# A branch hint, an earlier flag, later weight splits and y copies on ScalarE alone, in a kernel of attention, expert routing and a gated layer

## The chip, the cores and the metric

The kernel runs on one core of a Trainium2 chip. The metric is the device time of one execution in microseconds (us), as the median of several runs. Five engines work side by side, each with its own instruction queue: TensorE (PE; its weight loads are PEld), VectorE (DVE), ScalarE (ACT), GpSimd (POOL) and SyncE (SP), which issues DMAs. A name with q behind it (DVEq, SPq) is an instruction that the engine's sequencer handles itself: a wait, a branch, a DMA issue.

## What is computed

Three stages, one after the other, in float32:

```python
attn_out = _attn_ref(q, k, v)                     # 4 batches, 8 heads, 576 positions, 64 wide; two window masks
x = attn_out.transpose(0, 2, 1, 3).reshape(2304, 512)

logits = x @ w_gate                               # 8 experts
for idx in np.argsort(-logits.flatten()):         # greedy: best pairs first
    tok, e = idx // 8, idx % 8
    if assigned[tok] >= 0 or counts[e] >= 288:    # every expert takes 288 tokens
        continue
    assigned[tok] = e; counts[e] += 1
out[mask_e] = np.maximum(x[mask_e] @ w1[e], 0) @ w2[e]

gate = 1 / (1 + np.exp(-(out @ moe2_w_gate)))     # 1536 wide
return (gate * (out @ moe2_w_val)) @ moe2_w_out
```

## The kernel before

**Stages.** Attention runs up to about 105 us of the profiled execution. It writes its rows to the DRAM tensor xrows and leaves the logits on the chip. Routing follows (`Route.settle`, L591 to L609), then the expert phase (`Dense.phase_m`, L857), then the gated layer (`Dense.phase_g`, L984). The program is scheduled by hand: on each engine, instructions run in the order in which they are traced, and the framework adds the waits.

**Routing.** `settle` makes five rounds of a bidding scheme (`update`, `choice`), after which a flag says whether more are needed. `count` (L535) writes the number of tokens of each expert into `TB[:, 0]` and each token's place into `TB[:, 1]`; both, and `idxp`, are parts of one PSUM tile, rmisc. `positions` (L556) turns places into row numbers: VectorE makes tables, 18 matmuls (L575) add them up into `idxp`, and two VectorE instructions (L576, L577) make `rows`. `gather` then issues three indirect DMAs on GpSimd (L793), each bringing 128 rows of x (256 KB) for the first expert, and `check` (L543 to L554, seven VectorE instructions) makes a flag that says whether the five rounds were not enough. Every engine loads the flag (L589) and branches (L605). In the rare path, which these inputs don't take, further rounds and a general search follow, and then `positions` and `gather` again. `warm` (L463) issues filler matmuls on TensorE; W2 is 13 of them.

**Weights of the experts.** There are 64 steps, eight for each of eight experts. A step's weights (512 KB, `fetch`, L736, on SP) land in one of four raw buffers; ScalarE makes the high half (`high`, L742), VectorE the low half (`low`, L747), and the low half frees the raw buffer for a later fetch. Three steps stand ready before the expert phase: their high halves are made ahead of `settle`, and `fill` makes the low halves and fetches three further steps. `fill` stands between `check` and the branch.

**A step of the expert phase** (`phase_m`): perhaps a gather and a turn (L801, L811, L812) for the next expert, then `l1` of step j (12 matmuls, L824; ScalarE's relu, L828; VectorE's low half, L829), `l2` of step j - 2 (12 matmuls, L846, into four PSUM tiles y0 to y3 that exist once), `high` and `low` of step j + 2, `feed`, and a fetch of step j + 6. Behind an expert's last `l2` the four y tiles are copied to the SBUF tile yo, two by VectorE and two by ScalarE (L850), and ScalarE issues the store to DRAM (L851). The next expert's first `l2` writes the same PSUM tiles; between the two lies one `l1`.

**Weights of the gated layer.** `enter(t, p)` (L894) fetches a piece p (512 KB, L752, on SP) and enters it for conversion at step t + 3; `feed` converts it (`conv_g`, L755: four VectorE instructions and one of ScalarE) and splits it a step later (`split_g`, L769: one of each). Nine pieces are needed before `phase_g` begins. Three are entered ahead of `settle` (L1118) for steps 3, 5 and 7; six at steps 3, 9, 15, 21, 27 and 33 of `phase_m`.

Of the kernel before, what the change touches and what calls it, by code (L numbers as in the profile page):

```python
# [18 lines left out]
NT, DM, E, CAP = 2304, 512, 8, 288  # L19
# [349 lines left out]
W0, W1, W2, WA, WB = 10, 8, 13, 6, 5  # L369
# [44 lines left out]
class Route:  # L414
# [138 lines left out]
            nc.vector.tensor_copy(f[:, 1:2], f[:, 2:3])  # L553
        nc.vector.tensor_tensor(out=self.flag, in0=f[:, 0:1], in1=f[:, 1:2], op=ALU.add)  # L554

    def positions(self, rows):  # L556
        nc = self.nc
        S, slot, pg, M2, og = self.S, self.slot, self.pg, self.M2, self.og
        nc.vector.tensor_tensor(out=S, in0=self.TB[:, 1], in1=self.He, op=ALU.mult)
        with nc.allow_low_precision("slot numbers are small integers"):  # L560
            nc.vector.tensor_reduce(out=slot[:, 0], in_=S.rearrange("p e c -> p c e"), axis=AX.X, op=ALU.add)
        nc.vector.tensor_scalar(out=slot[:, 1], in0=slot[:, 0], scalar1=127, scalar2=None, op0=ALU.bitwise_and)
        nc.vector.tensor_scalar(out=slot[:, 2], in0=slot[:, 0], scalar1=-128, scalar2=None, op0=ALU.bitwise_and)
        nc.vector.tensor_copy(pg, slot[:, 1:3])
        pf, gf = pg[:, 0], pg[:, 1]
        nc.vector.tensor_tensor(out=og, in0=gf.unsqueeze(1).to_broadcast([128, NCH, NCH]), in1=self.gid, op=ALU.is_equal)
        nc.gpsimd.tensor_tensor(out=M2[:, 0], in0=og, in1=self.cid, op=ALU.mult)
        nc.scalar.activation(out=M2[:, 1], in_=og, func=AF.Copy, scale=self.pid)
        for c0 in (0, HC):
            nc.vector.tensor_tensor(out=self.G[:, :, c0:c0 + HC], in0=pf[:, c0:c0 + HC].unsqueeze(1).to_broadcast([128, 128, HC]),  # L570
                                    in1=self.tab[:, 4], op=ALU.is_equal)
        M2v = M2.rearrange("p a g c -> p (a g) c")
        out = self.idxp.rearrange("p a g -> p (a g)")
        for c in range(NCH):
            nc.tensor.matmul(out, self.G[:, :, c], M2v[:, :, c], start=(c == 0), stop=(c == NCH - 1))  # L575
        nc.vector.tensor_scalar(out=self.ip, in0=self.idxp, scalar1=128.0 * (NCH - 1), scalar2=None, op0=ALU.min)  # L576
        nc.vector.scalar_tensor_tensor(out=rows, in0=self.ip[:, 1], scalar=127.0, in1=self.ip[:, 0], op0=ALU.min, op1=ALU.add)  # L577

# [12 lines left out]
    def settle(self, rows, gather, fill, segments=(5, 1, 2)):  # L591
        s = 0
        for _ in range(segments[0]):
            self.update(s, s == 0, s == segments[0] - 1)
            self.choice()
            s += 1
        self.count()
        self.warm(W1)
        self.positions(rows)
        gather()  # L600
        self.warm(W2)
        self.check(segments[0], False)
        fill()
        v = self.load_flag()
        with self.tc.If(v > 0):  # L605
            self.more(s, segments[1:])
            self.count()
            self.positions(rows)
            gather()  # L609

    def more(self, s, segments):
        if not segments:
# [112 lines left out]
class Dense:  # L725
# [63 lines left out]
    def gather(self, c):  # L789
        if c not in self.xg:  # L790
            self.xg[c] = self.xgp.tile([128, DM], F32, tag="xg", name="xg")
        t = self.xg[c]
        self.nc.gpsimd.indirect_dma_start(out=t, out_offset=None, in_=self.xrows,  # L793
                                          in_offset=bass.IndirectOffsetOnAxis(ap=self.rows[:, c:c + 1], axis=0))
# [40 lines left out]
    def l2(self, j):  # L835
        nc = self.nc
        e, f = divmod(j, 8)
        wh, wl = self.hl.pop(j)
        hh, hl = self.h.pop(j)
        if e not in self.ya:  # L840
            self.ya[e] = self.out_tiles()
        y = self.ya[e]
        for m in range(4):
            s = slice(512 + 128 * m, 640 + 128 * m)
            for n, (w, x) in enumerate(((wh, hh), (wh, hl), (wl, hh))):
                nc.tensor.matmul(y[m], w[:, s], x, start=(f == 0 and n == 0), stop=(f == 7 and n == 2))  # L846
        if f == 7:
            t = self.yp.tile([128, 4, CAP], F32, tag="yo", name="yo")
            for m in range(4):
                (nc.scalar.copy if m % 2 else nc.vector.tensor_copy)(t[:, m], y[m])  # L850
            nc.scalar.dma_start(out=self.yd[:, :, CAP * e:CAP * e + CAP], in_=t)  # L851
            del self.ya[e], self.xt[e]

    def chunks(self, e):
# [2 lines left out]
    def phase_m(self, ng):  # L857

        J = 8 * E
        nc = self.nc  # L860
        gq = [(f, i) for f in range(ng) for i in range(3)][3:]
        self.ya[0] = self.out_tiles()
        for c, n in zip(self.chunks(0), HEAT):
            self.turn(c)
            for _ in range(n):
                nc.tensor.matmul(self.ya[0][0][:, 0:256], self.identb[:, 0:128], self.identb)
        for j in range(J + LAG):
            e, f = divmod(j, 8)
            if e + 1 < E:
                cs = list(self.chunks(e + 1))  # L870
                if 1 <= f <= len(cs):
                    self.gather(cs[f - 1])
                if 4 <= f < 4 + len(cs):
                    self.turn(cs[f - 4])
            if j < J:
                self.l1(j)
            if j >= LAG:
                self.l2(j - LAG)
            if AHEAD <= j + 2 < J:
                self.high(j + 2)  # L880
                self.low(j + 2)
            self.feed(j)
            if J - 4 <= j < J - 2:
                self.fetch_y(0, j - J + 4)
            if J - 2 <= j < J:
                self.split_y(0, 0, j - J + 2)
            if j + AHEAD + 3 < J and j:
                self.fetch(j + AHEAD + 3)
            if j % 6 == 3 and gq:
                self.enter(j, gq.pop(0))  # L890
        for d in range(LAG, 6):
            self.feed(J + d)
# [134 lines left out]
def body(tc, *args):  # L1027
    with ExitStack() as top:
        program(tc, top, *args)


def program(tc, top, qh, kh, vh, wgate, cst, csb, wm, wgv, out):
    nc = tc.nc
    with tc.manual_schedule():
# [9 lines left out]
        rows = cp.tile([128, NCH], I32, name="rows")  # L1044
        toks = cp.tile([128, NCH], I32, name="toks")
        dn = Dense(tc, raw, wm, wgv)
        with ExitStack() as rt:
# [60 lines left out]
            def gather():  # L1108
                for c in dn.chunks(0):
                    dn.gather(c)  # L1110
# [4 lines left out]
                    dn.fetch(j + 4)  # L1115

            dn.rawg = pool(mring, "rawg", 3, side="right")
            for i in range(3):  # L1118
                dn.enter(2 * i, (0, i))
            r.settle(rows, gather, fill)  # L1120
            r.tokens(toks)
        NG0 = 3
# [43 lines left out]
```

## Time and profile before

| | us |
|---|---|
| Runs of the kernel before | 832.21, 825.86, 830.13; median 830.13 |
| The profiled execution, own time | 833.87 |
| Its span, first to last instruction | 831.9 |
| TensorE busy in the span | 796.3 |
| VectorE, ScalarE, GpSimd busy | 470.0, 328.0, 66.8 |

Times in the rows below count from the first instruction of the profiled execution. A row of a timeline has the start, the duration, engine, line and operation, what is written and read, and behind it in brackets how long the engine was idle before and what ended that. Instructions of the same kind that follow each other are merged (x3); some records of matmuls are missing. [...]

### The profile page before, as it was taken

To read this page: it belongs to the slowest core of one execution; us is meant where nothing else is said; L and a number is where in the kernel's file an instruction comes from. 1 tells how busy PE (TensorE), PEld (TensorE's weight loads), DVE (VectorE), ACT (ScalarE), POOL (GpSimd) and SP (SyncE) were. 2 spreads that over 40 slices of the span, in tenths; PEclk is the share of its full clock that TensorE was granted. 3 is DMA by queue.
4 is the path that set the end of the run, shared out by engine and by line. 5 is a ranking of instruction groups with operands and counts; after the bars stand their busy time and mean duration, and the time that the engine had idled before them with its cause. 6 is when DMAs were issued, how large, how long until landed. Compare 5 with 4: busy or idle time off the path is not lost.

```text
span 831.9 us, 14443 instructions
## 1 busy us (share of the span) xinstructions
PE 796.3 (96%) x5740; PEld 733.6 (88%) x5744; DVE 470.0 (56%) x930; ACT 328.0 (39%) x658; POOL 66.8 (8%) x110
## 2 busy tenths in 40 slices
PE   8789987898999999999999999999999999999997
PEld 5677854798999999999999999999999999999996
DVE  6779867496767665557554543454655543333322
ACT  6879710354555554445332333332322222212210
POOL 4223001201001100000000000000000000111002
PEclk9999969798999999999999999999999999999999
DMA  9789620555766665554312221113222101121002
GB/s 250 205 234 263 200 79 21 177 192 199 223 214 227 224 217 183 173 181 142 89 53 81 70 82 39 45 45 89 70 67 98 39 20 39 58 76 39 24 14 76
DMA packets 51152, 100.24 MB, mean 120 GB/s; under 512 B 4952, under 2 KB 34296, under 8 KB 51080
## 3 DMA queue, kind: packets, MB, share of 16 engines
q1 hardware_dynamic: 43736, 84.91, 34.1%
q0 software_dynamic: 2976, 9.54, 3.2%
q10 hardware_dynamic: 4368, 4.82, 1.7%
q8 instruction: 47, 0.77, 0.4%
q14 instruction: 25, 0.20, 0.1%
HBM read 85.09 MB, written 14.16 MB: 119 GB/s over the span
## 4 chain that ended last, share of the span: by engine, by line
PE 78%; DVE 2%; DMA 1%; issue 0%; ACT 0%; POOLq 0%; ACTq 0%; POOL 0%; another core or an unknown queue 0%; DVEq 0%
PE gv L942 36%; PE o L964 18%; PE hps L824 12%; PE y L846 11%; DMA xg<-xrows,rows 1%; PE xps L801 1%; DVE wlo L747 1%; ACT whi L742 0%; DVE cx L763 0%; DVE cx L764 0%; DVE hl L829 0%; DVE yo L850 0%; DVE gw L778 0%; POOLq L1162 0%; ACTq L851 0%
## 5 line engine op out<-in xcount | busy, mean ns | idle before, releaser
L942 PE MATMUL gv<-yhi,gw 128*128 128x384 f32 x1152 | 304.9, 335 | 0.0
L942 PEld LDWEIGHTS gv<-yhi,gw 128*128 128x128 f32 x1152 | 209.2, 188 | 3.0
L942 PE MATMUL gv<-ylo,gw 128*128 128x384 f32 x576 | 192.9, 335 | 0.0
L947 DVE TENSOR_TENSOR sg<-sg,gv 128x384 f32<-128x384 f32 x72 | 39.9, 553 | 190.9 <-PE gv L942 190.9
L964 PE MATMUL o<-gw,ghi 128*128 128x512 f32 x432 | 134.3, 392 | 0.0
L942 PEld LDWEIGHTS gv<-ylo,gw 128*128 128x128 f32 x576 | 108.1, 188 | 3.0
L950 ACT CAST ghi<-sg 128x384 fp32r<-128x384 f32 x72 | 36.9, 512 | 163.9 <-DVE sg L947 163.9
L747 DVE TENSOR_TENSOR wlo<-raw,whi 128x1024 fp32r<-128x1024 f32 x64 | 78.1, 1223 | 30.7 <-ACT whi L742 30.7
L946 ACT ACTIVATE sg<-gv 128x384 f32<-128x384 f32 x72 | 35.4, 492 | 147.9 <-PE gv L942 147.7
L964 PEld LDWEIGHTS o<-gw,ghi 128*128 128x128 f32 x432 | 80.1, 188 | 13.4
L964 PE MATMUL o<-gw,glo 128*128 128x512 f32 x216 | 85.4, 396 | 0.0
L824 PE MATMUL hps<-xh,wlo 128*128 128x288 f32 x256 | 77.6, 303 | 1.1 <-DVE wlo L747 1.1
L824 PE MATMUL hps<-xh,whi 128*128 128x288 f32 x256 | 78.2, 306 | 0.1
L846 PE MATMUL y<-hh,whi 128*128 128x288 f32 x256 | 76.2, 298 | 2.2 <-DVE yo L850 2.2
L846 PE MATMUL y<-hh,wlo 128*128 128x288 f32 x256 | 76.1, 297 | 0.0
L846 PE MATMUL y<-hl,whi 128*128 128x288 f32 x256 | 76.0, 297 | 0.0
L824 PE MATMUL hps<-xl,whi 128*128 128x288 f32 x256 | 75.7, 296 | 0.0
L742 ACT CAST whi<-raw 128x1024 fp32r<-128x1024 f32 x64 | 66.5, 1041 | 9.1 <-DVE yo L850 6.1
L951 DVE TENSOR_TENSOR glo<-sg,ghi 128x384 fp32r<-128x384 f32 x72 | 40.2, 559 | 41.7 <-ACT ghi L950 41.7
L978 POOL DMA_INDIRECT out_dram<-acc,toks x18 | 17.5, 974 | 502.5 <-DVE acc L976 477.2
L828 ACT ACTIVATE hh<-hps 128x288 fp32r<-128x288 f32 x64 | 26.3, 412 | 69.3 <-PE hps L824 69.2
L824 PEld LDWEIGHTS hps<-xh,wlo 128*128 128x128 f32 x256 | 48.8, 191 | 3.0 <-DVE wlo L747 2.6
(153 smaller groups left out, 1137.0 us busy)
## 6 DMA issues: line engine op xcount, KB each, us to landing
raw<-in_moe_dram SPq DMA_DIRECT2D x100, 512.0 KB
raw<-yd SPq DMA_DIRECT2D x28, 384.0 KB
v<-in_v_dram SPq DMA_DIRECT2D x16, 292.5 KB
yd<-yo ACTq DMA_DIRECT2D x8, 576.0 KB
k<-in_k_dram SPq DMA_DIRECT2D x11, 384.0 KB
q<-in_q_dram SPq DMA_DIRECT2D x8, 384.0 KB
xrows<-x SPq DMA_DIRECT2D x18, 128.0 KB
v<-in_v_dram SPq DMA_DIRECT2D x8, 195.0 KB
```

Source lines behind the costliest of these rows:

```text
L742: self.nc.scalar.copy(hi, self.raw[j])
L747: self.nc.vector.tensor_tensor(out=lo, in0=self.raw.pop(j), in1=hi.bitcast(F32), op=ALU.subtract)
L824: nc.tensor.matmul(ps, w[:, 128 * k:128 * k + 128], x[:, k], start=(n == 0), stop=(n == 11))
L828: nc.scalar.activation(out=hi, in_=ps, func=AF.Relu)
L846: nc.tensor.matmul(y[m], w[:, s], x, start=(f == 0 and n == 0), stop=(f == 7 and n == 2))
L942: nc.tensor.matmul(p, w[:, a, s], x, start=(m == 0), stop=(m == 11))
L946: nc.scalar.activation(out=sg, in_=ps[0], func=AF.Sigmoid)
L947: nc.vector.tensor_tensor(out=sg, in0=sg, in1=ps[1], op=ALU.mult)
L950: nc.scalar.copy(hi, sg)
L951: nc.vector.tensor_tensor(out=lo, in0=sg, in1=hi.bitcast(F32), op=ALU.subtract)
L964: nc.tensor.matmul(self.oa[step][t], x[:, s], w[:, a, 1024:1536], start=(i == 0 and q == 0), stop=(i == FB - 1 and q == 2))
L978: st = nc.gpsimd.indirect_dma_start(out=self.out, out_offset=bass.IndirectOffsetOnAxis(ap=self.toks[:, c:c + 1], axis=0), in_=acc, in_offs ...
```

## The change

`check` is called inside `positions`, behind the 18 matmuls and ahead of the two instructions that make the row numbers. The part from `positions` to the rare path becomes a block of its own, at whose head each engine gets a hint that the branch labelled "settled" (around the rare path) is likely taken. Every engine loads the flag ahead of the filler matmuls W2. `fill` moves behind the branch. The three pieces of the gated layer's weights that were entered ahead of `settle` are entered in `phase_m`, and all nine now come at steps 8, 14, 20, ... 56. The four y tiles are copied by ScalarE alone, and SP issues the store.

```diff
-    def positions(self, rows):
+    def positions(self, rows, between=lambda: None):
...
             nc.tensor.matmul(out, self.G[:, :, c], M2v[:, :, c], start=(c == 0), stop=(c == NCH - 1))
+        between()
         nc.vector.tensor_scalar(out=self.ip, in0=self.idxp, scalar1=128.0 * (NCH - 1), scalar2=None, op0=ALU.min)
         nc.vector.scalar_tensor_tensor(out=rows, in0=self.ip[:, 1], scalar=127.0, in1=self.ip[:, 0], op0=ALU.min, op1=ALU.add)
...
         self.count()
         self.warm(W1)
-        self.positions(rows)
-        gather()
-        self.warm(W2)
-        self.check(segments[0], False)
+        with self.tc.block():
+            self.tc.mark_branch_hint_location("settled", "LikelyTaken", list(mybir.ALL_ENGINES))
+            self.positions(rows, lambda: self.check(segments[0], False))
+            gather()
+            v = self.load_flag()
+            self.warm(W2)
+            with self.tc.If(v > 0, label="settled"):
+                self.more(s, segments[1:])
+                self.count()
+                self.positions(rows)
+                gather()
         fill()
-        v = self.load_flag()
-        with self.tc.If(v > 0):
-            self.more(s, segments[1:])
-            self.count()
-            self.positions(rows)
-            gather()
...
             for m in range(4):
-                (nc.scalar.copy if m % 2 else nc.vector.tensor_copy)(t[:, m], y[m])
-            nc.scalar.dma_start(out=self.yd[:, :, CAP * e:CAP * e + CAP], in_=t)
+                nc.scalar.copy(t[:, m], y[m])
+            nc.sync.dma_start(out=self.yd[:, :, CAP * e:CAP * e + CAP], in_=t)
...
-        gq = [(f, i) for f in range(ng) for i in range(3)][3:]
+        gq = [(f, i) for f in range(ng) for i in range(3)]
...
-            if j % 6 == 3 and gq:
+            if j % 6 == 2 and j > 6 and gq:
                 self.enter(j, gq.pop(0))
...
             dn.rawg = pool(mring, "rawg", 3, side="right")
-            for i in range(3):
-                dn.enter(2 * i, (0, i))
             r.settle(rows, gather, fill)
```

## Rows read from the trace of the kernel before

**Rows 1.** The page: span, and the chain that ended last, by engine.

```profile
span 831.9 us, 14443 instructions
...
PE 78%; DVE 2%; DMA 1%; issue 0%; ACT 0%; POOLq 0%; ACTq 0%; POOL 0%; another core or an unknown queue 0%; DVEq 0%
```

**Rows 2.** Stretches: length, busy PE, PEld, DVE, ACT, POOL (x), PEclk, DMA share, GB/s.

```profile
143.70:148.00 4.30, 0.00 (x0) 0.02 (x1) 2.36 (x3) 0.00 (x0) 2.88 (x2) 0.77 0.87 252
146.02:156.26 10.24, 6.72 (x29) 5.19 (x30) 3.06 (x10) 1.92 (x4) 3.72 (x4) 0.50 0.70 238
...
160.00:190.39 30.39, 28.23 (x214) 27.88 (x213) 26.01 (x40) 16.14 (x29) 2.12 (x2) 1.00 0.53 174
190.39:197.22 6.83, 6.42 (x27) 5.91 (x26) 4.22 (x6) 4.01 (x6) 0.00 (x0) 0.50 0.79 261
...
155.00:374.70 219.70, 216.27 (x1599) 213.82 (x1598) 146.64 (x209) 110.33 (x181) 14.29 (x13) 0.98 0.62 198
```

**Rows 3.** TensorE's waits, 155 to 250 us: total us, times, longest.

```profile
PE y L846 <- DVE yo L850: 2.2, 1, 2.2
PE hps L824 <- DVE wlo L747: 1.1, 2, 0.7
```

**Rows 4.** Timeline of the end of routing, 134 to 156 us.

```profile
135.74 0.22 PE L541 MATMUL rmisc<-rH,rone 128*128 128x144 bf16 x1
...
136.00 0.31 DVE L559 TENSOR_TENSOR pS<-rmisc,rH 128x144 f32<-128x144 f32 x1 [0.38 <-PE rmisc L541]
...
140.88 0.20 DVE L576 TENSOR_SCALAR pip<-rmisc 128x36 f32<-128x36 f32 x1 [0.93 <-PE rmisc L575]
140.90 2.79 PE L463 MATMUL L<-const-bfloat16-1.0 128*128 128x512 bf16 x12
141.11 0.18 DVE L577 SCALAR_TENSOR_TENSOR rows<-pip 128x18 int32<-128x18 f32 x1
141.21 0.29 DVE L545 TENSOR_REDUCE rn<-rmisc 1x8 f32<-1x144 f32 x1
...
142.30 1.06 POOL L793 DMA_INDIRECT xg<-xrows,rows  x1 [3.26 <-DVE rf L549]
...
142.48 0.15 DVE L554 TENSOR_TENSOR rflag<-rf 1x1 int32<-1x1 f32 x1
142.56 3.50 DVE L747 TENSOR_TENSOR wlo<-raw,whi 128x1024 fp32r<-128x1024 f32 x3
...
143.81 2.60 SPq L736 DMA_DIRECT2D raw<-in_moe_dram  x3
...
148.01 1.08 PE L801 MATMUL xps<-ident,xg 128*128 128x128 f32 x4 [4.32 <-DVEq L605]
...
155.03 0.59 PE L824 MATMUL hps<-xh,whi 128*128 128x288 f32 x1
```

**Rows 5.** The branch, L605, by engine: ns min/median/max, first and last start.

```profile
L605 ACTq EVENT_SEMAPHORE  x2: 17/17/17, 143.7 to 143.7; - x2
...
L605 DVEq EVENT_SEMAPHORE  x2: 21/21/21, 147.9 to 148.0; - x2
...
L605 DVEq COMPARE_BRANCH  x1: 72/72/72, 143.4 to 143.4; - x1
```

**Rows 6.** The third gather in the chain; the first gather's time to landing.

```profile
144.95 8.14 DMA xg<-xrows,rows
...
DMA to landing us min/median/max: 4.3/4.3/4.3
```

**Rows 7.** Timeline of VectorE and of ScalarE at the first expert's end.

```profile
188.71 0.81 DVE L850 COPY yo<-y 128x288 f32<-128x288 f32 x2
...
190.25 1.05 ACT L742 CAST whi<-raw 128x1024 fp32r<-128x1024 f32 x1 [4.35 <-DVE yo L850]
```

**Rows 8.** Groups, 160 to 365 us: total us, mean ns, idle before.

```profile
L850 ACT COPY yo<-y 128x288 f32<-128x288 f32 x14 | 5.5, 400 | 4.6 <-PE y L846 4.6
...
L763 DVE SCALAR_TENSOR_TENSOR cx<-raw,cx 128x512 int32<-128x512 int32 x9 | 6.2, 693 | 0.3
```

## The prediction

> **What bounds the kernel now.** I read the page's chain first: TensorE carries 78% of the 831.9 us span and every other engine 2% or less [rows 1], so the change can only win where TensorE waits or runs slowly. Next the stretches with their granted clock, to find those places. [...] Then TensorE's waits from 155 to 250: 2.2 us for a copy of y made by VectorE, and 1.1 us in two waits for a low half of a weight [rows 3]. Last the timeline of the end of routing, where the branch is.
>
> There the reader is to see two chains. The first is the branch. The flag is ready at 142.63. VectorE branches at 143.4 and runs the first instruction behind the branch at 147.9; ScalarE is past its branch at 143.7 [rows 4, 5]. VectorE's own queue was empty at 142.56 + 3.50 = 146.06, so it did not wait for its own work. TensorE's first transpose, released by VectorE's 147.9, starts at 148.01 after 4.32 us of standing still [rows 4]. The second chain is the gathers: row numbers at 141.29, first gather 142.30, third gather issued 144.95 and landed 8.14 later, at 153.09; the first matmul of the experts starts at 155.03 [rows 4, 6]. The second chain ends last. So what the stall behind the branch costs by itself is nothing as long as the third gather lands where it does; removing it uncovers the gather.
>
> **Part 1: flag ahead of the row numbers.** The seven instructions of the check run from 141.21 to 142.63, 1.42 us, today behind the row numbers and so beside the gathers [rows 4]. They move between the position matmuls and the two instructions that make the row numbers. What decides is when they may start. They read the count in the PSUM tile rmisc, and the matmuls traced ahead of them write another part of the same tile. If the wait goes by bytes, they start when VectorE is free (140.88 - 0.93 = 139.95), end at 141.37, and the row numbers come 0.49 us later than now. If it goes by the tile, they start at 140.88 and the row numbers come 1.42 us later. The nearest row is L559: it multiplies what two earlier matmuls wrote, yet it started 0.04 us after the third, L541, which writes another part of the same tile [rows 4]. I take 1.42 and keep 0.49 for the range.
>
> [...]
>
> What is queued behind: all three gathers (first gather 1.01 us after the row numbers [rows 4]), so they start near 143.7, 145.1 and 146.4. TensorE's 13 filler matmuls (W2; the row has 12 of them) are now traced behind its own load of the flag; the flag comes only 0.33 us earlier than now (142.30), the branch follows some 0.8 us later as on VectorE today, so they start 2 us later than today's 140.90 and end near 145.6. TensorE's standing still changes from one piece of 4.3 us to two pieces of about 2 and 2.4. I price the clock at no change; that is the widest unknown of the sum. Today the half-clock stretch covers 1.23 us of expert work (155.03 to 156.26). If it slid to cover 10.24 us of it, half of the further 9.0 would be lost, 4.5; if it went away, 0.6 would be won.
>
> **Part 2: hint, and splits and loads behind the branch.** The hint adds one instruction per engine ahead of the positions; no row shows one, the nearest is a branch of 72 ns [rows 5], so 0 to 0.1 us on a chain that waits on semaphores anyway: I take 0. If it works VectorE goes on near 143.9 instead of 147.9. The three low halves (3.50 us) then run from about 144.1 to 147.6 and the three weight loads on SP, each waiting for one of them, begin about 1.6 us later than today's 143.81 [rows 4]. They delay the gathers today: the first gather took 4.3 us to land, the third 8.14 [rows 6]. As gathers and loads move by nearly the same amount (1.4 and 1.6), I expect the third to land 1.4 later, near 154.5, and the experts to start near 156.4. Bound the other way: a third gather that took only 4.3 would land 3.8 earlier, a net gain of 2.4. Cost of parts 1 and 2: **+1.4**, bounds -2.4 and +5.9 (1.4 + 4.5).
>
> **Part 3: gate weights.** Three loads, conversions and splits leave the start of the expert phase; all nine now enter at steps 8, 14, ... 56. One is five VectorE operations near 0.69 us [rows 8], some 3.2 us. VectorE was busy 26.0 of 30.4 us between 160 and 190, against 67% over the phase [rows 2], and only at 188.71 did it come to the y copies that TensorE waited 2.2 us for [rows 3, 7]. With no conversion before step 11, that queue is gone. The last one is split at step 60 of 64, ahead of the gate stage that needs it; late in the phase VectorE has room. Cost 0; if that room were gone, TensorE would wait at the start of the gate stage.
>
> **Part 4: y copied by ScalarE, stored by SP.** Per expert, two more ScalarE copies of 0.40 us [rows 8], 0.8 us, on an engine busy 110.3 of 219.7 [rows 2]; two copies leave VectorE. They hide behind the 12 matmuls of the next first layer, 12 x 0.135 = 1.6 us (216.27 / 1599 [rows 2]). ScalarE no longer holds its queue until VectorE's copies are done: that wait kept a weight cast back 4.35 us [rows 7] and so caused the 1.1 us of waits for low halves. On SP the store stands ahead of a weight load that waits for a later low half anyway: 0.
>
> **Sum.** Parts 3 and 4 remove the 2.16 us wait, the 1.1 us, and the half clock that followed the 2.16: 6.83 us at half clock with TensorE busy 6.42 of them lost 3.2 [rows 2, 3]. -2.2 - 1.1 - 3.2 + 1.4 = **-5.1 us**. The profiled execution took 833.87 us (span 831.9 plus 2.0 around it), so 828.8 for such a one; it stands 3.7 above the median of 830.13, so I forecast **825.0**. By the bounds of parts 1 and 2 it is 821.2 to 829.5.
>
> **Rivals.**
> - *The flag is made beside the matmuls* (wait by bytes): row numbers 0.49 later, 0.9 less: 824.1. L559 speaks against it. Chance 0.10.
> - *The hint does nothing.* VectorE goes on at 147.9 as today. The weight loads then start near 149.1, behind all three gathers; the third lands near 146.4 + 4.3 = 150.7. The experts then start 1.94 later as today (155.03 - 153.09), at 152.6, or later, as VectorE reaches the splits of x only behind the low halves, after 147.9 + 3.5 = 151.4; between 152.6 and the forecast's 156.4 I take 154.2, 2.2 before the forecast: 822.8. For it: nothing in the trace shows a hinted branch. Chance 0.17. *The hint works and the gathers still land in 4.3*: experts start 3.8 earlier, 821.2. Chance 0.06.
> - *The queue at 187 stays* (the wait and the half clock return a step later through the conversion at step 11): only 1.1 or nothing is won, 1.4 lost: 831.5. Against it: VectorE has 11 steps free ahead of it. Chance 0.12.
> - *Slower: ScalarE is late with y.* Four copies (1.6), a weight cast, a square and a relu meet where an expert's end and a conversion fall together (steps 17 and 41); if y comes over 1.6 us late, TensorE waits as at 187, and each such place costs 2.16 + 3.2 = 5.4. One place brings 830.4, level with now; from two on the change is slower: 835.7. For it: ScalarE's copies stand in order behind its other work. Against it: it is half idle. Chance 0.10.
> - The forecast: 0.45.
>
> **How the numbers follow.** 819 to 832 takes in the forecast with its bounds, the two rivals near it, the hint's two cases and the stalled one; most of the slower rival lies outside. 1% (8.3 us) is about what a measurement of this kernel can tell from no change. Faster by more, below 821.8: half of the hint's two cases (0.12) and the lower edge of the forecast (0.06), 0.18. Slower by more, above 838.4: half of the slower rival and a little for the clock, 0.07. Within: 0.75.
>
> **What would show it.** Right: no wait of TensorE for yo, clock 1.0 from 160 on, VectorE's first instruction behind the branch within 0.6 us of it, row numbers near 142.7, the experts' first matmul near 156.4. Wrong: row numbers at 141.8, a branch that still takes 4 us on VectorE, half clock inside the expert phase, or a TensorE wait for ScalarE's y copies.

## The result, and the profile after

The changed kernel took 819.58 us (median of four runs, 818.06 to 820.97) beside 830.52 us of the kernel before (four runs, 825.86 to 832.21): ratio 0.9877, interval 0.9833 to 0.9921, so 10.9 us less, with an interval from 6.6 to 13.9. I had forecast 5.1 less. The profiled execution took 820.97 us.

The page of the changed kernel, span and chain by engine:

```profile
span 818.9 us, 14454 instructions
...
PE 80%; DMA 1%; DVE 1%; ACT 0%; issue 0%; POOLq 0%; POOL 0%; SPq 0%; DVEq 0%
```

TensorE carries 80% where it carried 78 [rows 1], and the span is 13.0 us shorter. I cut both spans at three points of TensorE: the end of the 18 position matmuls, the first matmul of the experts and the first of the gated layer.

| stage, us | before | after | difference |
|---|---|---|---|
| start to the end of the position matmuls | 140.85 | 138.45 | -2.40 |
| from there to the first expert matmul | 14.18 | 12.35 | -1.83 |
| expert phase | 219.53 | 210.37 | -9.16 |
| gated layer | 451.16 | 451.52 | +0.36 |
| tail | 6.22 | 6.22 | 0 |

The first line is code that the change leaves alone (but for the hint, and the three early gate loads); over all fourteen traces of this study it lies between 135.82 and 143.46, whether the change is in or not. I leave it out. What is left is 1.83 + 9.16 - 0.36 = 10.6 us, close to the difference of the medians.

Stretches of the changed kernel (columns as in rows 2; PEclk is the mean granted TensorE clock as a share of full speed, and half clock is a PEclk of 0.50): around the branch, the whole expert phase, and the first expert's part of it.

```profile
139.56:146.38 6.82, 5.33 (x12) 1.78 (x12) 2.12 (x6) 0.00 (x0) 3.00 (x3) 0.50 0.37 110
...
150.80:361.16 210.36, 210.36 (x1598) 210.12 (x1597) 140.79 (x194) 116.22 (x197) 14.37 (x13) 1.00 0.65 211
...
160.00:190.39 30.39, 30.39 (x233) 30.39 (x233) 18.28 (x25) 16.69 (x28) 3.50 (x3) 1.00 0.71 220
```

The expert phase has nothing left to win: TensorE is busy 210.36 of 210.36 us at full clock, where it was 216.27 of 219.70 at 0.98 [rows 2]. VectorE is busy 18.3 us in the first expert's stretch, where it was 26.0 [rows 2]. The half clock is still there, but under the filler matmuls (139.6 to 146.4) and no longer under expert work.

The end of routing in the timeline of the changed kernel, to be laid beside rows 4:

```profile
136.69 1.76 PE L575 MATMUL rmisc<-pM,rG 128*128 128x36 bf16 x18 [1.39 <-POOL pM L567]
...
138.49 0.29 DVE L545 TENSOR_REDUCE rn<-rmisc 1x8 f32<-1x144 f32 x1 [0.92 <-PE rmisc L575]
...
139.76 0.15 DVE L554 TENSOR_TENSOR rflag<-rf 1x1 int32<-1x1 f32 x1
...
140.05 0.18 DVE L578 SCALAR_TENSOR_TENSOR rows<-pip 128x18 int32<-128x18 f32 x1
...
140.84 5.33 PE L463 MATMUL L<-const-bfloat16-1.0 128*128 128x512 bf16 x12 [2.39 <-DVE rows L578]
...
141.23 1.06 POOL L795 DMA_INDIRECT xg<-xrows,rows  x1 [4.59 <-ACTq L606]
...
143.88 0.96 POOL L795 DMA_INDIRECT xg<-xrows,rows  x1 [0.31 <-remote]
...
144.83 3.49 DVE L749 TENSOR_TENSOR wlo<-raw,whi 128x1024 fp32r<-128x1024 f32 x3 [4.61 <-DVEq L606]
...
146.09 2.60 SPq L738 DMA_DIRECT2D raw<-in_moe_dram  x3
...
146.73 0.63 PE L803 MATMUL xps<-ident,xg 128*128 128x128 f32 x4 [0.56 <-PEq L606]
...
149.78 0.66 PE L803 MATMUL xps<-ident,xg 128*128 128x128 f32 x4 [1.23 <-DVE xl L814]
...
150.80 0.40 PE L826 MATMUL hps<-xh,whi 128*128 128x288 f32 x1
```

Three things are to be seen. The check begins 0.04 us after the 18 matmuls (138.49, they end at 138.45), not when VectorE came free 0.92 us earlier, and the row numbers come 1.77 us behind the matmuls instead of 0.45. VectorE still stands idle for 4.61 us until it is past its branch, and with it stand the low halves and the three weight loads: 146.09 is 7.64 us behind the matmuls, where it was 2.96. And the gathers no longer end last: the last transposes before the experts wait 1.23 us for VectorE's split of x.

The same last transposes in the kernel before:

```profile
153.23 1.08 PE L801 MATMUL xps<-ident,xg 128*128 128x128 f32 x4 [0.84 <-DMA xg<-xrows,rows]
```

They start 12.38 us behind the position matmuls there and 11.33 in the changed kernel: 1.05 of the 1.83 us. The other 0.78 is the clock: from these transposes to the first expert matmul it took 1.80 us at half clock [rows 2] and takes 1.02 at full clock.

Two rows of ScalarE at the first expert's end answer to rows 7:

```profile
179.58 1.58 ACT L852 COPY yo<-y 128x288 f32<-128x288 f32 x4
...
181.06 1.05 ACT L744 CAST whi<-raw 128x1024 fp32r<-128x1024 f32 x1
```

The four copies take 1.58 us and the weight cast follows without the 4.35 us of standing still.

### The profile page after: what moved, and what is told of

The parts are those of the page before. It is cut to its first block, busy times and chain, and to the rows that moved or that the text cites. A ratio compares the mean times of both kernels' runs of the same rounds, so it can differ in the third digit from the quotient of the medians.

```text
span 818.9 us, 14454 instructions
## 1 busy us (share of the span) xinstructions
PE 789.8 (96%) x5740; PEld 728.1 (89%) x5744; DVE 465.0 (57%) x914; ACT 334.0 (41%) x674; POOL 65.8 (8%) x110
## 4 chain that ended last, share of the span: by engine, by line
PE 80%; DMA 1%; DVE 1%; ACT 0%; issue 0%; POOLq 0%; POOL 0%; SPq 0%; DVEq 0%
PE gv L944 36%; PE o L966 18%; PE hps L826 12%; PE y L848 12%; PE xps L803 1%; DMA raw<-in_moe_dram 1%; DVE wlo L749 0%; ACT yo L852 0%; ACT L948 0%; POOLq L1162 0%; POOL out_dram L980 0%; DVE acc L978 0%; ACT cm L767 0%; DVE xl L814 0%; PE y L868 0%
## 5 line engine op out<-in xcount | busy, mean ns | idle before, releaser
L826 PE MATMUL hps<-xh,wlo 128*128 128x288 f32 x256 | 75.9, 297 | 0.0
L826 PEld LDWEIGHTS hps<-xl,whi 128*128 128x128 f32 x256 | 48.4, 189 | 0.1
```

Source lines behind the costliest of these rows:

```text
L826: nc.tensor.matmul(ps, w[:, 128 * k:128 * k + 128], x[:, k], start=(n == 0), stop=(n == 11))
```

## The experiments

In the tables that follow, times are us from the end of the position matmuls to: the row numbers, the first and third gather's issue, VectorE's arrival at the branch, the start of the weight loads, the first expert matmul. "Gap" is the time from VectorE's branch to its first instruction behind it.

**One part alone.** Three kernels: the y copies alone on the kernel before, the gate weights alone on the kernel before, and the changed kernel with both undone, which leaves the branch's part (its edits are those below, turned round).

```diff
@@ y only
-                (nc.scalar.copy if m % 2 else nc.vector.tensor_copy)(t[:, m], y[m])
-            nc.scalar.dma_start(out=self.yd[:, :, CAP * e:CAP * e + CAP], in_=t)
+                nc.scalar.copy(t[:, m], y[m])
+            nc.sync.dma_start(out=self.yd[:, :, CAP * e:CAP * e + CAP], in_=t)
@@ gate weights only
-        gq = [(f, i) for f in range(ng) for i in range(3)][3:]
+        gq = [(f, i) for f in range(ng) for i in range(3)]
-            if j % 6 == 3 and gq:
+            if j % 6 == 2 and j > 6 and gq:
-            for i in range(3):
-                dn.enter(2 * i, (0, i))
```

> The kernel before with part 4 alone (four y tiles copied by ScalarE, store on SP). Measured from the first expert matmul to the first gate matmul the kernel before takes 219.5 us and the changed one 210.4. Theory (y copies are what TensorE waited for, and ScalarE's wait for VectorE's copies made its weight casts late): TensorE's wait for y and the half clock behind it go although the early conversions stay, and so do the small stops at each expert's end: 210.5 to 213, the whole run 6 to 9 us faster than before. Rival (VectorE's queue of early conversions is the cause, and it then holds up the low halves instead): 216 to 219, 0 to 3 us faster. From the end of the position matmuls to the first expert matmul both expect no change, 14.2.

> The kernel before with part 3 alone (nine pieces of gate weights entered at steps 8, 14 ... 56). Theory: the wait for y at the first expert's end and the half clock behind it go, the stops for low halves at each expert's end stay: 212 to 214 from first expert matmul to first gate matmul, 5 to 7 us faster than before. Rival (the wait for y comes back at a later expert's end, where a conversion and the copies meet, steps 17 and 41): a wait of 1 to 2 us for y by VectorE there, again followed by half clock, 217 to 220, within 2 us of before.

> The changed kernel with parts 3 and 4 undone, so the kernel before with parts 1 and 2 (flag ahead of the row numbers, hint, block, weight splits and loads behind the branch, filler matmuls behind the flag). Theory: 12.4 us from the end of the position matmuls to the first expert matmul (14.2 before), because the loads no longer share the DMA engines with the gathers; the expert phase as before, 219, with the wait for y; the whole 1 to 3 us faster. Rival (the flag ahead costs what was forecast and the profiled run of the change was lucky): 15 to 16 us there, the whole 0 to 2 us slower.

| | median, ratio [interval] | to experts | expert phase | gaps in it | TensorE busy at half clock in it |
|---|---|---|---|---|---|
| before | | 14.18 | 219.53 | 3.43 | 1.23 + 6.42 |
| y only | 825.57, 0.9940 [0.9907, 0.9974] | 14.15 | 213.31 | 0.83 | 3.12 |
| gate weights only | 824.11, 0.9947 [0.9917, 0.9977] | 14.09 | 213.54 | 0.62 | 1.31 |
| branch only | 825.45, 0.9941 [0.9913, 0.9969] | 12.29 | 218.30 | 4.04 | 3.05 |
| after | 819.58, 0.9877 [0.9833, 0.9921] | 12.35 | 210.37 | 0 | 0 |

As expected, either of parts 3 and 4 removes the 2.16 us wait by itself, and the half clock behind it. (By the ratios the whole runs are 5.0, 4.4 and 4.9 us faster; 6 to 9, 5 to 7 and 1 to 3 were expected.) So they don't add: one alone takes 6.2 or 6.0 us off the expert phase, both together 9.2. What only both remove is seen in TensorE's waits, those of its weight loads (PEld) for the low halves, first of the kernel before (155 to 375 us), then y only and gate weights only (150 to 365 us):

```profile
PEld hps L824 <- DVE wlo L747: 2.6, 7, 1.0
```

```profile
PEld hps L824 <- DVE wlo L747: 1.0, 2, 0.8
```

```profile
PEld hps L824 <- DVE wlo L747: 2.5, 9, 0.4
```

The changed kernel has no such row. The matmul behind a late weight load shows as one of longer duration (0.40 us beside 0.29 and 0.30 of its neighbours at 221.36 in the kernel before, where the load had waited 0.17), so part of the wait is missing from a list of TensorE's gaps. Take the gaps, and half of the busy time at half clock (an estimate: in the kernel before, such matmuls follow each other every 0.24 us from 193.01 on and every 0.13 from 189.45 to 190.25), from each expert phase: 219.53 - 3.43 - 3.83 = 212.3 before, 212.3 with gate weights only, 212.7 with the branch only, 210.9 with y only, 210.4 after. Those 1.9 to 2.3 us above the changed kernel go with the y copies, not with the gate weights.

The branch alone has the old wait (the first row, TensorE's waits) and no half clock behind it (the second, a stretch from 183.80):

```profile
PE y L848 <- DVE yo L852: 2.2, 1, 2.2
```

```profile
183.80:190.60 6.80, 5.79 (x41) 5.33 (x42) 4.48 (x7) 4.16 (x6) 0.00 (x0) 1.00 0.61 200
```

The same stop was followed by 6.83 us at half clock in the kernel before [rows 2] and by none here. So the 3.2 us that the forecast gave to it are not there in every such trace.

**The hint.** One line out of the changed kernel, and the same line moved, in the source, from ahead of the positions to just ahead of the flag's load.

```diff
@@ no hint, and hint late
-            self.tc.mark_branch_hint_location("settled", "LikelyTaken", list(mybir.ALL_ENGINES))
             self.positions(rows, lambda: self.check(segments[0], False))
             gather()
@@ hint late, behind gather()
+            self.tc.mark_branch_hint_location("settled", "LikelyTaken", list(mybir.ALL_ENGINES))
             v = self.load_flag()
```

> The changed kernel without the hint, all else as changed. Theory (the hint fetches nothing; in the changed trace no instruction packet moved between the hint and the branch): VectorE's first instruction behind the branch again 3.8 to 4.5 us after it, 12 to 13 us from the end of the position matmuls to the first expert matmul, the same time as the changed kernel within 1 us. Rival (the hint takes part of the fetch away, 4.5 to 3.9): VectorE's gap is 4.5 and the experts start 0.6 later or more.

> The changed kernel with the hint moved from the head of the block to just ahead of the loading of the flag. Theory (the hint fetches nothing, wherever it stands): VectorE's first instruction behind the branch 3.6 to 3.9 us after it, first expert matmul 12 to 13 us after the end of the position matmuls. Rival (the hint works when it is close enough to the branch): the gap is below 1.5 us; then the low halves and the loads start 2.5 us earlier, the gathers share with them, and the experts start later, near 15.

VectorE's branch (the lower row) and what follows it (the upper row) in the changed kernel, without a hint, and with the line moved:

```profile
L606 DVEq EVENT_SEMAPHORE  x2: 21/21/21, 144.5 to 144.7; - x2
...
L606 DVEq COMPARE_BRANCH  x1: 84/84/84, 140.7 to 140.7; - x1
```

```profile
L605 DVEq EVENT_SEMAPHORE  x2: 21/21/21, 143.8 to 143.9; - x2
...
L605 DVEq COMPARE_BRANCH  x1: 72/72/72, 140.2 to 140.2; - x1
```

```profile
L606 DVEq EVENT_SEMAPHORE  x2: 21/21/21, 142.1 to 142.2; - x2
...
L606 DVEq COMPARE_BRANCH  x1: 84/84/84, 138.6 to 138.6; - x1
```

The gap is 3.86 us with the hint, 3.61 without, 3.43 with the line moved. Without it the whole kernel took 820.41 us (ratio 0.9892, interval 0.9855 to 0.9930), level with the changed one. Moving the line did not move the instruction. VectorE's hint with the line moved:

```profile
L1162 DVEq BRANCH_PREFETCH_HINT  x1: 56/56/56, 130.6 to 130.6; - x1
```

That is 5.8 us ahead of the end of the position matmuls (136.40), where the changed kernel has it 5.7 ahead (its row is below), and VectorE runs the same instructions in the same order in both. So this run (818.46 us) is a second execution of the changed kernel. It shows what two executions differ by: 0.43 in the gap, and 0.44 in the start of the experts (11.91 for 12.35). The 3.61 without a hint lies between the two; a hint nearer to the branch is not tested. VectorE's hint did run in the changed kernel, 7.9 us ahead of the branch. Its row, then the DMA view of the 4 us behind it, then of the 4 us behind the branch (packets, MB and share of the two queues that the view marks "instruction"):

```profile
L1162 DVEq BRANCH_PREFETCH_HINT  x1: 56/56/56, 132.8 to 132.8; - x1
```

```profile
DMA packets 0, 0.00 MB, mean 0 GB/s; under 512 B 0, under 2 KB 0, under 8 KB 0
```

```profile
q14 instruction: 4, 0.03, 3.0%
q8 instruction: 1, 0.02, 1.5%
```

No packet of any kind behind the hint, five of instructions behind the branch (the view has the packets of all engines, and each of them branches there). Between the two windows, ahead of the branch, one instruction packet moves, at 136.89 (the expectation for the kernel without a hint has none there); the kernel before, which has no hint, has one in the same place, 1.6 us ahead of the end of the position matmuls in both. That VectorE's gap is the time in which these packets bring it the code behind the branch is my reading; no run shows it, since the view has all engines together. Nor does any run show why VectorE's hint brought nothing.

**The flag's place.** The changed kernel with the check behind the row numbers again.

```diff
-            self.positions(rows, lambda: self.check(segments[0], False))
+            self.positions(rows)
+            self.check(segments[0], False)
             gather()
```

> The changed kernel with the check behind the two instructions that make the row numbers, as before, still inside the block and ahead of the branch. All times count from the end of the position matmuls. Theory (the flag ahead delays rows and gathers by the whole check, since both read one PSUM tile with the matmuls, and what ends last in the changed kernel is VectorE behind the branch): row numbers at 0.45 instead of 1.77, gathers from 1.45 instead of 2.78, flag at 1.78 instead of 1.45, so VectorE's branch, its low halves and the first expert matmul 0.3 later than in the changed kernel, 12.6 to 12.8. Rival (the gathers end last there): the experts start earlier, 11 to 11.5.

The row numbers came 0.44 behind the matmuls, 1.33 earlier than in the changed kernel, so the price of part 1 was close to the forecast's 1.42; and yet the experts started 1.21 later, at 13.56, where 12.6 to 12.8 was expected; one run took 823.42 us. VectorE's branch in this kernel, and its last turn:

```profile
L607 DVEq EVENT_SEMAPHORE  x2: 21/21/21, 146.9 to 147.0; - x2
...
L607 DVEq COMPARE_BRANCH  x1: 84/84/84, 142.1 to 142.1; - x1
```

```profile
152.21 0.66 PE L804 MATMUL xps<-ident,xg 128*128 128x128 f32 x4 [2.16 <-DVE xl L815]
```

The gap is 4.85 where it was 3.86, and the branch is reached 0.20 later: 1.19 together, as much as the loss. The gathers had time to spare, VectorE had none. Over the fourteen traces the gap is 4.30 to 4.85 in six of the seven whose first gather was issued ahead of VectorE's branch (before, y only, gate weights only, this one, and two below). It is 3.13 in the seventh, which reaches its branch only at 6.49, and 2.67 to 3.91 in the seven that have the first gather behind the branch. Part of the difference lies ahead of the first instruction packet. In the changed kernel that packet comes 0.9 us behind VectorE's branch; here it comes 1.5 behind, and in the first 1.42 us behind the branch (142.08 to 143.50) only the gather's queue moves packets:

```profile
q0 software_dynamic: 35, 0.14, 39.8%
```

Whether the gather held up the instruction packets, no run here tests: it is a correlation.

**Low halves ahead of the branch.** First with the loads, which is close to the order that the forecast thought it would get (low halves and loads soon, gathers 1.33 late); this kernel also goes without the block. Then the low halves alone ahead of the branch and the loads behind it; then the same with the check behind the row numbers.

```diff
@@ fill in front
         gather()
+        fill()
         v = self.load_flag()
...
-        fill()
@@ lows in
             gather()
+            lows()
             v = self.load_flag()
...
-            def fill():
+            def lows():
                 for j in range(AHEAD):
                     dn.low(j)
+
+            def fill():
+                for j in range(AHEAD):
                     dn.fetch(j + 4)
@@ lows in, flag late: lows in, and
-            self.positions(rows, lambda: self.check(segments[0], False))
+            self.positions(rows)
+            self.check(segments[0], False)
```

> The changed kernel with the low halves and the three weight loads ahead of the branch again (and without the block, whose form does not allow them inside). Theory (the change wins at the branch because the weight loads no longer share the DMA engines with the gathers): loads start 4.3 us after the end of the position matmuls instead of 7.6, the third gather lands 7 to 8 us after its issue, the first expert matmul at 15 to 16 instead of 12.4, half clock reaching into the expert phase. Rival (what wins is the order of the flag and the filler matmuls): 12 to 13.

> The changed kernel with the three low halves ahead of the branch, inside the block, and the three loads left behind it. Theory (VectorE waits 3.6 to 3.9 us for its code behind the branch with nothing queued, and low halves and token numbers behind it hold up the splits of x): the low halves run in that gap; if the loads still start after 7 us, the third transposes no longer wait for VectorE and the first expert matmul comes at 10.5 to 11.5. If the loads start at once at 4 to 5 us instead, the gathers share with them and it comes at 14 to 16.

> The same as the run before, with the check behind the row numbers as well. Theory: row numbers and gathers 1.3 us earlier; if the loads stay behind the gathers the first expert matmul comes at 9.5 to 11, some 1.5 to 3 us less than the changed kernel, the whole at 0.984 to 0.988 of before. If the loads start at 4 to 5 us, 13 to 15 and no gain on the changed kernel.

| | rows | gathers | branch, gap | loads | experts | expert phase | us |
|---|---|---|---|---|---|---|---|
| after | 1.77 | 2.78, 5.43 | 2.23, 3.86 | 7.64 | 12.35 | 210.37 | 819.58 |
| flag late | 0.44 | 1.45, 4.09 | 2.43, 4.85 | 8.82 | 13.56 | 210.37 | 823.42 |
| fill in front | 1.78 | 2.78, 6.34 | 2.55, 2.67 | 2.94 | 15.51 | 210.17 | 823.64 |
| lows in | 1.78 | 2.78, 6.36 | 2.58, 3.30 | 3.09 | 15.22 | 211.06 | 822.89 |
| lows in, flag late | 0.44 | 1.45, 4.11 | 2.61, 4.72 | 3.41 | 13.36 | 211.92 | 821.63 |

The last column is a median of four runs in the first and the last row and a single run in the others; the argument goes by the columns before it.

Fill in front, timeline and then a row of the chain:

```profile
141.06 2.60 SPq L737 DMA_DIRECT2D raw<-in_moe_dram  x3
...
142.27 1.88 POOL L794 DMA_INDIRECT xg<-xrows,rows  x1 [0.30 <-DVE wlo L748]
...
150.24 1.12 PE L802 MATMUL xps<-ident,xg 128*128 128x128 f32 x4 [3.35 <-DMA xg<-xrows,rows]
```

```profile
142.27 7.92 DMA xg<-xrows,rows
```

With the loads beside the gathers, a gather takes 7.92 us and TensorE waits 3.35 for it; the experts start at 15.51, where the forecast's arithmetic had 156.4 - 140.85 = 15.55. That the two agree so closely is partly chance: the loads start at 2.94, where the forecast had them near 4.6, and the gather that TensorE waits for longest is the second, not the third. The loads were expected at 4.3 and half clock inside the expert phase; neither came. In "lows in" the loads wait only for the low halves, since SP passes its own branch in little time (0.56 us in the changed kernel, 140.82 to 141.38), and the collision stayed (15.22). With the check late as well, the gathers lead the loads by more and the turns still wait for a gather:

```profile
140.78 2.79 SPq L740 DMA_DIRECT2D raw<-in_moe_dram  x3
...
149.75 0.63 PE L805 MATMUL xps<-ident,xg 128*128 128x128 f32 x4 [2.42 <-DMA xg<-xrows,rows]
```

Timed, it is 0.9903 (interval 0.9865 to 0.9940): nothing over the changed kernel.

**Fillers ahead of the flag's load**, as in the kernel before, in the changed kernel.

```diff
-            v = self.load_flag()
             self.warm(W2)
+            v = self.load_flag()
```

> The changed kernel with the filler matmuls W2 ahead of the loading of the flag again. They then run beside the check, some 3 us at full clock from 0.1 after the position matmuls, and TensorE stands still from 3 to 6 or 7. Theory (the place of W2 is worth little, VectorE's gap sets the start of the experts): the first expert matmul at 12 to 13, but a longer half-clock stretch over the first experts, up to 2 us more in the expert phase. Rival (W2 behind the flag at half clock holds up the first transposes): experts start at 11 to 11.8.

823.87 us in one run; experts at 13.25. TensorE stands still in one piece again, and half clock then covers its turns and the first expert matmuls (a stretch from 145.10, then the last transposes):

```profile
145.10:155.30 10.20, 7.33 (x32) 6.20 (x33) 6.27 (x12) 1.92 (x4) 4.47 (x5) 0.50 0.85 274
```

```profile
151.41 1.12 PE L803 MATMUL xps<-ident,xg 128*128 128x128 f32 x4 [1.35 <-DVE xl L814]
```

The last transposes start at 11.42, 0.09 later than in the changed kernel, and wait for VectorE as they do there; but from them to the first expert matmul it takes 1.83 us instead of 1.02. The expert phase takes 211.11, 0.74 more than in the changed kernel. So the place of the fillers is worth some 1.6 us in these two traces. In the changed kernel the fillers themselves run at half clock (12 in 5.33 us at a PEclk of 0.50, before 12 in 2.79 [rows 4] at 1.00) and the clock is back ahead of the experts.

**Loads behind the turns.** Two kernels in which ScalarE issues the three weight loads behind the first expert's three turns, when the gathers are down. The first also has the check late, and the low halves and the token numbers ahead of the branch. The second is the kernel before with this edit alone.

```diff
@@ both, ahead of the loop over the steps
+        for j in range(AHEAD):
+            self.fetch(j + 4, nc.scalar)
@@ the first, in settle
-            self.positions(rows, lambda: self.check(segments[0], False))
+            self.positions(rows)
+            self.check(segments[0], False)
             gather()
+            lows()
             v = self.load_flag()
@@ the first, lows in place of fill
                 for j in range(AHEAD):
                     dn.low(j)
-                    dn.fetch(j + 4)
+                r.tokens(toks)
@@ the second, fill
                 for j in range(AHEAD):
                     dn.low(j)
-                    dn.fetch(j + 4)
```

> Built on the changed kernel: check behind the row numbers, low halves and token numbers ahead of the branch so that VectorE does them in its gap, and the three loads issued by ScalarE behind the first three turns (at about 11 us). Theory (loads that share with the gathers are the whole cost, and VectorE's gap holds nothing else up): gathers at 1.45 to 4.1 land within 4.5, third transposes at 8.3 to 9.3, first expert matmul at 9.7 to 10.7 against 12.35, the expert phase 210 to 212; the whole at 0.983 to 0.986 of before, 2 to 3 us below the changed kernel. Rival (the late loads keep the experts waiting for weights): stops for high or low halves of steps 4 to 6, the expert phase 213 or more.

> The kernel before with one edit: the three loads are issued by ScalarE behind the first three turns. Theory (the third gather, slowed by the loads, ends last in the kernel before): the third gather lands near 8.5 us after the end of the position matmuls instead of 12.3, TensorE's first transposes wait for VectorE's gap as before (7.0), the first expert matmul at 10.5 to 11.5 instead of 14.2, the whole at 0.994 to 0.997 of before. Rival (VectorE's gap behind the branch ends last by itself): 13 or more.

The first missed what was expected of it: 822.41 us (0.9903, interval 0.9867 to 0.9938), experts at 12.78. No turn waits for a gather any more, but with the low halves and the token numbers ahead of it VectorE reaches its branch 6.49 us behind the matmuls and stands 3.13 us there, and TensorE's first turn waits for that:

```profile
142.85 3.50 DVE L751 TENSOR_TENSOR wlo<-raw,whi 128x1024 fp32r<-128x1024 f32 x3
...
150.85 0.63 PE L805 MATMUL xps<-ident,xg 128*128 128x128 f32 x4 [1.79 <-DVEq L608]
```

The second is the test of what the changed branch brought, without moving the branch, the flag or the hint:

```profile
143.19 1.08 PE L801 MATMUL xps<-ident,xg 128*128 128x128 f32 x4 [2.86 <-DVEq L605]
...
146.41 0.62 PE L801 MATMUL xps<-ident,xg 128*128 128x128 f32 x4
...
147.38 0.40 PE L824 MATMUL hps<-xh,whi 128*128 128x288 f32 x1
...
147.75 1.31 ACTq L736 DMA_DIRECT2D raw<-in_moe_dram  x3
```

No turn waits for a gather, and the experts start at 11.56, 2.62 earlier than in the kernel before and 0.79 earlier than in the changed one, with a gap of 4.66 and the row numbers at 0.44. (10.5 to 11.5 was expected.) The kernel took 824.75 us (0.9957, interval 0.9926 to 0.9988), within what was expected of it. Its expert phase still has the 2.16 us wait, again with no half clock behind it, and takes 217.14. This edit together with parts 3 and 4 might start the experts 0.8 us earlier than the changed kernel does; it was not run, and two executions of one kernel differed by 0.44 there.

## Why the prediction was right in places and low in sum

- **What bounds it, parts 3 and 4: right, under-sized.** The 2.16 us wait, the queue of VectorE, the held weight cast and the half clock were the places, and all are gone. The term was -6.5 (-2.2 - 1.1 - 3.2). Measured are gaps of 3.43 for 3.26, 3.2 for the half clock, and 1.9 that the sum lacks (9.16 - 3.43 - 3.2, and 0.6 of half clock at the phase's start that belongs to the branch). The 1.9 stands where the weight loads came late; I had listed TensorE's waits and not those of its weight loads, and a matmul that waited for its weights looked busy (0.40 us at 221.36 in the kernel before, beside 0.29 and 0.30). Which part does what I had in one term: each removes the big wait alone, and the late weight loads go with the y copies.
- **Part 1, the flag: right.** The row numbers came 1.33 later for 1.42, and the wait went by the PSUM tile here, not by addresses: L545 started 0.04 us after the matmuls. L559, which had started 0.04 us after L541, gave the right side. Wrong was to think that the delay reaches the experts: in the one trace with the late flag they started later, not earlier.
- **Part 2, the hint: the step that failed.** "If it works VectorE goes on near 143.9 instead of 147.9", and with it "gathers and loads move by nearly the same amount". The gap stayed (3.86), so the loads moved by 4.68 and the gathers by 1.33; they no longer met, and the start came at 12.35 instead of 15.55, a term of -1.83 instead of +1.37 (rounded to +1.4 there); 0.78 of the -1.83 is the clock's. The rival "the hint does nothing" had the mechanism, down to VectorE as what ends last, and a start at 13.35; its bounds were 11.75 to the forecast. Its 0.17 was too little: an instruction that no trace had shown was given the benefit of the doubt.
- **The clock: mis-sized.** Priced at no change, and it gave back 1.4 us: 0.78 between the last transposes and the first expert matmul, 0.6 in the first matmuls of the experts. TensorE's two stops were 2.39 and 0.56 us for the forecast's 2 and 2.4, because the fillers between them ran at half clock for 5.33 us; full clock was granted again at 146.38, ahead of the first turn at 146.73. The forecast named half clock sliding into the experts as its widest unknown. That happened in the kernel with the branch part only (3.05 us) and with the fillers ahead, among others, not in the changed one.
- **The slower rival** did not occur: no wait for ScalarE's copies of y. Nor did the queue at 187 come back.
- **The sum**: -5.1 - 3.2 (start, from +1.37 to -1.83) - 0.6 (clock at the start) - 0.2 (gaps) - 1.9 (weight loads) + 0.4 (gated layer) = -10.6. The 819.58 lies inside the range of 819 to 832, at its edge, and below the 821.8 that bounds "faster by over 1%", to which I had given 0.18. That it lies inside at all, by 0.6 us, is luck in part: the gain is about twice the forecast's, and at the branch it came by the path of a rival with a chance of 0.17. The forecast of a lost 1.4 at the branch, a clock priced at nothing, and parts 3 and 4 priced by TensorE's gaps alone all held the sum up.

What stays open: which of the traces get half clock behind a stop of 2.16 us, why the gap at the branch is longer in most traces that issue a gather ahead of it, and whether a hint nearer to the branch would shorten it.

## What to carry to other kernels

A stall of an engine that is not the bound can be worth keeping: here VectorE's 3.86 us at a branch, moved ahead of the weight loads, kept these off three gathers on which the next stage had waited. Order the transfers on purpose (with the loads behind the first turns, one edit, the experts started 2.6 us earlier) rather than by what happens to be late. Moving a line in the source need not move the instruction: look for it in the trace before reading the result. And when waits of TensorE are priced, list those of its weight loads too: here a matmul behind a late weight load counted as busy (0.40 us beside 0.30).

## What the runs showed of the hardware that I had not expected

VectorE's branch hint brought no packet of any kind within 4 us in the changed kernel (none from 132.7 to 136.7). VectorE's gap was 3.86 and 3.43 us in two executions of the changed kernel, with its hint some 8 us ahead of the branch, and 3.61 without. The gap itself was 2.67 to 4.85 us over fourteen traces. A gather of 128 rows took 8.14 and 7.92 us to land beside three weight loads of 512 KB (the third of the kernel before, the second of fill in front); in the kernel before with its loads moved last, no turn waited for a gather. The same stop of TensorE, 2.16 us at the first expert's end, was followed by 6.83 us at half clock (PEclk 0.50) in the kernel before and by none (PEclk 1.00) with the branch part only and in the kernel before with its loads moved last.
